# Normalised rational polynomials and a three-product forward step in a fused FFT convolution and MLP

## The chip, the cores and the metric

The kernel runs on one core of a Trainium2 chip. The time is the device time of one execution in microseconds (us); several runs are taken and their median is quoted. A unit of work below is a piece of the MLP, not a unit of time.

## The reference

`x` is [8, 3008, 256], two filters are [1505, 256]. Per batch and channel the sequence is filtered in the frequency domain, then every token goes through an MLP whose activation is a rational function:

```python
X = np.fft.rfft(x, axis=1)
y = np.fft.irfft(X * (filt_r + 1j * filt_i)[None], n=3008, axis=1)     # tokens: 24064 x 256
h = y @ w_in                                                           # 256 -> 2048
P = a[0] + a[1] * h + a[2] * h**2 + a[3] * h**3
Q = 1.0 + abs(b[0]) * abs(h) + abs(b[1]) * h**2
out = (P / (Q + 1e-06)) @ w_out                                        # 2048 -> 256
```

## The kernel before

The transform of length 3008 = 64 x 47 is cut into steps. **Stage 1** folds the input and multiplies by a 47-point matrix (line 444 for batches 1 to 7). **Stage 2** works in 12 steps a batch: the forward 64-point product y (`product`, line 497, one float32 matmul of 128x512), the multiplication by the filter on VectorE (DVE, lines 501 and 502), a cross term and a sum on GpSimd (POOL, lines 517 and 521), a split of the result into two float32r halves (`halves`: the upper on ScalarE (ACT), line 527, the lower on POOL, line 528), and the inverse product z as three float32r matmuls (`product3`, line 358), which is copied out of PSUM by `evac`, line 353, on the engine that the string `EV2` names ("V": DVE). **Stage 3** (line 590) is the 47-point inverse; its result is split into the halves `xh` and `xl`.

The MLP has 752 units (47 tiles of 512 tokens by 16 slices of 128 hidden features; the last one is cut in two). A unit makes six float32r products h (lines 631 to 634), the activation, and six products o (lines 714 to 716). The activation is taken by completing squares: on ACT `act0` |h| (L639), `act1` (h+PC)² (L646), `act2` (|h|+QC)² (L652), `act3` the reciprocal root of q+QK (L657), `act4` its square (L667; from unit 624 on POOL for every other unit, L665). PC, QC, QK, PK, P0 are [128,1] columns of the tile `scal`. On POOL follow q+QK (L677) and q times the upper half of g (L696), on DVE `p` (L682), `g_hi` (L691), `rest` (L699) and `g_lo` (L705).

The order is written by hand: `pipeline` goes through the units, and in each iteration issues the products h of unit i, then one piece of the generator `conv_items` for the next batch (stage 1, four pauses, stage 2), then the products o of unit i-4 and the steps of `ORDER` for earlier units. A generator's `yield` with a cost hands back the turn until enough credit is there; a bare `yield` is a pause of one iteration. Batch 0 and the splitting of the weights are done in `head`, ahead of the first unit; there a planner (`Plan`) orders the steps of all engines by estimated durations and due times. The step `flag` (L217 to L223) tests the coefficients, `scalars` (`square_scalars`) works out the columns on POOL, and the MLP's body stands behind a branch on the flag.

Of the kernel before, what the change touches and what calls it, by code (L numbers as in the profile page):

```python
# [11 lines left out]
I32 = mybir.dt.int32  # L12
# [28 lines left out]
CPOS = 3  # L41
V2 = "A"
# [140 lines left out]
def conv_moe(ctx: ExitStack, tc: tile.TileContext, xp, filt, w_in, w_out, mats, small, sgn, outT):  # L183
# [27 lines left out]
    B0, B1 = (abs_sb[:, i : i + 1] for i in (4, 5))  # L211
    P0, PC, PK, QC, QK, SC = (col(i) for i in range(6))

    def load_flag():


        nc.scalar.activation(abs_sb, ab_sb, AF.Abs)  # L217
        sq, c = col(8, 2), col(10, 2)
        tt(out=sq, in0=ab_sb[:, 6:8], in1=ab_sb[:, 6:8], op=ALU.mult)
        tt(out=c, in0=abs_sb[:, 8:10], in1=abs_sb[:, 10:12], op=ALU.mult)  # L220
        stt(out=c, in0=c, scalar=16.0, in1=sq, op0=ALU.mult, op1=ALU.is_ge)
        stt(out=c, in0=abs_sb[:, 10:12], scalar=1e-6, in1=c, op0=ALU.is_ge, op1=ALU.mult)
        tt(out=flag_sb, in0=col(10), in1=col(11), op=ALU.mult)  # L223

    def square_scalars():

        g = nc.gpsimd
        ts, tt = g.tensor_scalar, g.tensor_tensor
        x, y, z = col(6, 2), col(8, 2), col(10, 2)
        for n, src in ((6, A3), (7, B1)):  # L230
            ts(out=col(n), in0=src, scalar1=1.0, scalar2=None, op0=ALU.mult)
        v.reciprocal(y, x)
        tt(out=z, in0=x, in1=y, op=ALU.mult)
        ts(out=z, in0=z, scalar1=-1.0, scalar2=2.0, op0=ALU.mult, op1=ALU.add)
        tt(out=y, in0=y, in1=z, op=ALU.mult)
        tt(out=SC, in0=A3, in1=col(9), op=ALU.mult)
        p1, q1, pc2, qc2 = (col(i) for i in range(10, 14))
        for out, a, r in ((PC, A2, col(8)), (QC, B0, col(9))):
            ts(out=pc2, in0=a, scalar1=0.5, scalar2=None, op0=ALU.mult)
            tt(out=out, in0=pc2, in1=r, op=ALU.mult)  # L240
        tt(out=P0, in0=A0, in1=col(8), op=ALU.mult)
        tt(out=p1, in0=A1, in1=col(8), op=ALU.mult)
        ts(out=q1, in0=col(9), scalar1=1.000001, scalar2=None, op0=ALU.mult)
        tt(out=pc2, in0=PC, in1=PC, op=ALU.mult)
        tt(out=qc2, in0=QC, in1=QC, op=ALU.mult)
        tt(out=PK, in0=p1, in1=pc2, op=ALU.subtract)
        tt(out=QK, in0=q1, in1=qc2, op=ALU.subtract)

# [202 lines left out]
    class Stage2:  # L451


        def __init__(self, b):
            self.b, self.f, self.tin, self.ev, self.z, self.sides, self.parts = b, {}, {}, {}, {}, {}, {}

# [155 lines left out]
    class Unit:  # L612


        def __init__(self, i, squares):
            self.i, self.squares = i, squares
            self.t, self.f, self.cols = units[i]
            self.p0 = P0 if squares else A0

# [24 lines left out]
        def act1(self):  # L644
            if self.squares:
                nc.scalar.activation(self.w, self.H, AF.Square, bias=PC)  # L646
            else:
                nc.scalar.activation(self.w, self.H, AF.Identity, scale=A3, bias=A2)

        def act2(self):  # L650
            if self.squares:
                nc.scalar.activation(self.q, self.q, AF.Square, bias=QC)  # L652

        def act3(self):
            if self.squares:
# [97 lines left out]
    def head():  # L753
# [266 lines left out]
    with tc.manual_schedule(engines=ENGINES):  # L1020
# [85 lines left out]
```

## Time and profile before

| what | value |
|---|---|
| median of 3 runs | 2480.59 us (2480.01 to 2483.05) |
| profiled execution, first to last instruction | 2480.0 us; the trace shows nothing around it |
| PE (TensorE) busy | 2431.0 us, 98% |
| ACT busy | 2348.5 us, 95% |
| DVE busy | 2277.8 us, 92% |
| POOL busy | 2089.9 us, 84% |
| mean busy share of the DMA engines | 27.0% |

An instruction's row gives its start and its duration. Successive instructions of one engine overlap at their ends, so the time that one takes from its engine is the distance between two starts where the engine did not wait; a busy time of many instructions is their union.

### The profile page before, as it was taken

What the parts mean: (1) busy time and instruction counts of PE and PEld (TensorE: products, weight loads), DVE (VectorE), ACT (ScalarE), POOL (GpSimd) and SP (SyncE); (2) the same over time, 40 slices, a digit from 0 to 9 for tenths busy, and PEclk for the clock granted to TensorE, in tenths of its full rate; (3) what the DMA queues carried; (4) which work ended last, traced back from release to release, by engine and by line L of the source; (5) the groups of instructions that cost most, each with busy time, mean ns of one, the idle gap of its engine ahead of it and who ended that gap; (6) DMA issues with size and microseconds to landing.
All of it is one profiled execution on the core that took longest, in us unless ns stands there. A gap on an engine that the chain in (4) does not pass through costs nothing.

```text
span 2480.0 us, 36386 instructions
## 1 busy us (share of the span) xinstructions
PE 2431.0 (98%) x10770; PEld 1941.0 (78%) x10770; DVE 2277.8 (92%) x3568; ACT 2348.5 (95%) x4178; POOL 2089.9 (84%) x2240
## 2 busy tenths in 40 slices
PE   7699999999999999999999999999999999999999
PEld 4577777878778787787787877878778788888887
DVE  7789988999899998999889998999889999999998
ACT  6799999999999999999999999999999999999998
POOL 7788887898879987899878997889879887888898
PEclk8899999999999999999999999999999999999999
DMA  7533332322323232332323322332222210100000
GB/s 260 151 111 108 94 106 84 102 85 72 108 90 93 85 87 73 110 90 83 95 79 102 92 80 80 95 103 90 86 79 85 68 37 17 34 26 17 21 9 19
DMA packets 102423, 205.15 MB, mean 83 GB/s; under 512 B 9455, under 2 KB 55855, under 8 KB 102215
## 3 DMA queue, kind: packets, MB, share of 16 engines
q1 hardware_dynamic: 102215, 202.74, 27.0%
q8 instruction: 87, 1.43, 0.2%
q14 instruction: 121, 0.99, 0.1%
HBM read 130.53 MB, written 72.17 MB: 82 GB/s over the span
## 4 chain that ended last, share of the span: by engine, by line
PE 76%; ACT 8%; POOL 6%; DVE 6%; issue 3%; DMA 1%; SPq 0%; DVEq 0%; POOLq 0%; ACTq 0%
PE o L715 11%; PE o L714 11%; PE o L716 11%; PE h_u L631 11%; PE h_u L632 11%; PE h_u L634 11%; PE s L444 3%; PE x L590 3%; POOL q_u L696 3%; PE y L497 2%; PE z L358 2%; ACT q_u L652 2%; ACT q_u L639 2%; POOL q_u L677 1%; ACT a_u L657 1%
## 5 line engine op out<-in xcount | busy, mean ns | idle before, releaser
L696 POOL TENSOR_TENSOR q_u<-q_u,hi_u 128x512 f32<-128x512 f32 x753 | 975.4, 1295 | 246.5 <-DVE hi_u L691 226.7
L714 PE MATMUL o<-hi_u,wo_sb 128*128 128x512 f32 x1506 | 661.4, 439 | 0.0
L691 DVE SCALAR_TENSOR_TENSOR hi_u<-h_u,scal,a_u 128x512 fp32r<-128x512 f32 x753 | 557.4, 740 | 52.4 <-ACT a_u L667 44.1
L631 PE MATMUL h_u<-xhl,wi_sb 128*128 128x512 f32 x1506 | 592.6, 394 | 6.1 <-DVE raw L325 4.0
L715 PE MATMUL o<-lo_u,wo_sb 128*128 128x512 f32 x1506 | 588.5, 391 | 7.9 <-DVE lo_u L705 7.7
L716 PE MATMUL o<-hi_u,wo_sb 128*128 128x512 f32 x1506 | 587.6, 390 | 0.0
L632 PE MATMUL h_u<-xhl,wi_sb 128*128 128x512 f32 x1506 | 587.3, 390 | 0.0
L699 DVE SCALAR_TENSOR_TENSOR h_u<-h_u,scal,q_u 128x512 f32<-128x512 f32 x753 | 563.7, 749 | 24.2 <-POOL q_u L696 22.9
L682 DVE SCALAR_TENSOR_TENSOR h_u<-w_u,scal,h_u 128x512 f32<-128x512 f32 x753 | 560.3, 744 | 5.2 <-ACT w_u L646 5.2
L657 ACT ACTIVATE a_u<-q_u,scal 128x512 f32<-128x512 f32 x753 | 549.3, 729 | 0.0
L652 ACT ACTIVATE q_u<-q_u,scal 128x512 f32<-128x512 f32 x753 | 547.2, 727 | 1.9
L677 POOL TENSOR_SCALAR q_u<-q_u,scal 128x512 f32<-128x512 f32 x753 | 525.5, 698 | 1.5 <-ACT a_u L657 1.4
L646 ACT ACTIVATE w_u<-h_u,scal 128x512 f32<-128x512 f32 x753 | 518.8, 689 | 0.0
L705 DVE TENSOR_TENSOR lo_u<-h_u,a_u 128x512 fp32r<-128x512 f32 x753 | 512.5, 681 | 0.1
L639 ACT ACTIVATE q_u<-h_u 128x512 f32<-128x512 f32 x753 | 453.6, 602 | 56.6 <-PE h_u L634 46.8
L634 PE MATMUL h_u<-xhl,wi_sb 128*128 128x512 f32 x1506 | 464.5, 390 | 0.0
L667 ACT ACTIVATE a_u<-a_u 128x512 f32<-128x512 f32 x688 | 438.4, 637 | 0.3
L715 PEld LDWEIGHTS o<-lo_u,wo_sb 128*128 128x128 f32 x1506 | 283.3, 188 | 97.7 <-issue 37.0
L714 PEld LDWEIGHTS o<-hi_u,wo_sb 128*128 128x128 f32 x1506 | 283.0, 188 | 88.8 <-issue 36.9
L631 PEld LDWEIGHTS h_u<-xhl,wi_sb 128*128 128x128 f32 x1506 | 283.3, 188 | 74.3 <-DVE lo_u L705 8.8
L632 PEld LDWEIGHTS h_u<-xhl,wi_sb 128*128 128x128 f32 x1506 | 283.4, 188 | 60.4 <-issue 1.3
L716 PEld LDWEIGHTS o<-hi_u,wo_sb 128*128 128x128 f32 x1506 | 282.6, 188 | 60.9
(94 smaller groups left out, 2221.8 us busy)
## 6 DMA issues: line engine op xcount, KB each, us to landing
f<-filt SPq DMA_DIRECT2D x168, 256.0 KB
xin<-xp SPq DMA_DIRECT2D x48, 512.0 KB
scr<-ev SPq DMA_DIRECT2D x48, 512.0 KB
outT<-oe SPq DMA_DIRECT2D x46, 512.0 KB
xin<-scr SPq DMA_DIRECT2D x42, 512.0 KB
scr<-xin SPq DMA_DIRECT2D x42, 480.0 KB
tl<-scr SPq DMA_DIRECT2D x96, 192.0 KB
tl<-scr SPq DMA_DIRECT2D x62, 96.0 KB
```

Source lines behind the costliest of these rows:

```text
L631: nc.tensor.matmul(o, w_in_part(0, f, cc), xh[:, cc, ts], start=cc == 0, stop=False)
L632: nc.tensor.matmul(o, w_in_part(0, f, cc), xl[:, cc, ts], start=False, stop=False)
L634: nc.tensor.matmul(o, w_in_part(1, f, cc), xh[:, cc, ts], start=False, stop=cc == 1)
L652: nc.scalar.activation(self.q, self.q, AF.Square, bias=QC)
L657: nc.scalar.activation(self.a, self.q, AF.Abs_reciprocal_sqrt, bias=QK)
L682: v.scalar_tensor_tensor(out=H, in0=w, scalar=PK, in1=H, op0=ALU.add, op1=ALU.mult)
L691: nc.vector.scalar_tensor_tensor(out=self.hi, in0=self.H, scalar=self.p0, in1=self.a, op0=ALU.add, op1=ALU.mult)
L696: nc.gpsimd.tensor_tensor(out=self.q, in0=self.q, in1=self.hi.bitcast(F32), op=ALU.mult)
L699: nc.vector.scalar_tensor_tensor(out=self.H, in0=self.H, scalar=self.p0, in1=self.q, op0=ALU.add, op1=ALU.subtract)
L714: nc.tensor.matmul(o, w_out_part(0, f, dd), self.hi, start=f == 0 and self.cols.start == 0, stop=False)
L715: nc.tensor.matmul(o, w_out_part(0, f, dd), self.lo, start=False, stop=False)
L716: nc.tensor.matmul(o, w_out_part(1, f, dd), self.hi, start=False, stop=f == 15 and self.cols.stop == T)
```

## The change

**The polynomials** are scaled so that every added constant is 1 or -1. `act1`, `act2` and `act3` take the immediate bias 1.0 and a scale from one of three ACT registers, loaded once behind the branch (`load_rates`). `g_hi` and `rest` add the immediate 1.0. On POOL `pool_q1` multiplies and adds with two columns (S1, S2) where it had the immediate 1.0 and one column. The factor that is left over goes into the matrix `e_sb` of stage 3 and into SC. The columns are worked out on DVE (`scale_scalars`, ahead of the sixth fold), and the flag has more conditions.

**The forward product** of batches 1 to 7 becomes three float32r products: a new method `split` makes the halves of a piece of the loaded tile, the upper on ACT, the lower on DVE, one step ahead of the product. Stage 2 begins with three more pauses.

**The rest**: `EV2` becomes "A" (z is copied out by ACT), the costs of y and z in credit fall from 0.86 to 0.68, the lower halves of the matrices are made on DVE, and a scratch area of SBUF is made smaller.

```diff
-EV1, EV2, EVO = "A", "V", "AV"
-XB, FB = 4, 3
+EV1, EV2, EVO = "A", "A", "AV"
+XB, FB, YB = 4, 3, 2
...
-    fwd_sb = consts.tile([128, 128], F32, name="fwd_sb")
+    fwd_sb = consts.tile([128, 2, 128], F32R, name="fwd_sb")
...
+    def load_rates():
+        for k in range(3):
+            rate.append(nc.scalar.alloc_register(f"rate{k}"))
+            nc.scalar.reg_load(rate[k], rates_sb[:1, k : k + 1].bitcast(I32))
...
+        def split(self, i):
+            q, j = divmod(i, 2)
+            y = self.flat(self.tin[q], j)
+            tile = conv.tile([128, 2, TT], F32R, tag="yr", name=f"yr{self.b}_{i}", bufs=YB)
+            hi, lo = self.halved[i] = tile[:, 0], tile[:, 1]
+            nc.scalar.activation(hi, y, AF.Copy)
+            tt(out=lo, in0=y, in1=hi.bitcast(F32), op=ALU.subtract)
...
         def product(self, i):
-            yield 0.86
+            yield 0.68
             bank, yt = banks.tile(f"y_{b}_{i}")
-            nc.tensor.matmul(yt, fwd_sb, self.flat(self.tin[q], j), start=True, stop=True)
+            product3(yt, fwd_sb, *self.halved.pop(i))
...
+        yield
+        yield
+        s.split(0)
+        yield
         for i in range(13):
             if i < 12:
                 yield from s.product(i)
+            if i < 11:
+                s.split(i + 1)
             if i > 0:
                 yield from s.inverse(i - 1)
...
-            self.p0 = P0 if squares else A0
+            self.p0 = 1.0 if squares else A0
...
-                nc.scalar.activation(self.w, self.H, AF.Square, bias=PC)
+                nc.scalar.activation(self.w, self.H, AF.Square, bias=1.0, scale=rate[0])
...
-                nc.scalar.activation(self.q, self.q, AF.Square, bias=QC)
+                nc.scalar.activation(self.q, self.q, AF.Square, bias=1.0, scale=rate[1])
...
-                    nc.scalar.activation(self.a, self.q, AF.Abs_reciprocal_sqrt, bias=QK)
+                nc.scalar.activation(self.a, self.q, AF.Abs_reciprocal_sqrt, bias=1.0, scale=rate[2])
...
-                nc.gpsimd.tensor_scalar(out=self.q, in0=self.q, scalar1=1.0, scalar2=QK, op0=ALU.mult, op1=ALU.add)
+                nc.gpsimd.tensor_scalar(out=self.q, in0=self.q, scalar1=S1, scalar2=S2, op0=ALU.mult, op1=ALU.add)
...
-        add("mats_lower", mats_lower, "POOL", 1.3, ["mats_upper"], due=61)
+        add("mats_lower", mats_lower, "DVE", 0.8, ["mats_upper"], due=61)
...
-        add("scalars", square_scalars, "POOL", 4.0, ["flag"], due=20, then=[])
+        add("scalars", scale_scalars, "DVE", 2.5, ["flag"], due=4)
```

How the instructions move, in the order in which each engine takes them (line numbers of each kernel, `x_u381` is the buffer of unit 381, `y_5_4` the product of step 4 of batch 5):

DVE in stage 2, around a forward product, before:

```order
L691 SCALAR_TENSOR_TENSOR hi_u382_14148<-h_u382_14071,scal_79,a_u382_14087 128x512
L501 TENSOR_TENSOR f25_2_13626<-y_5_4_14140,f25_2_13626 128x512
L502 TENSOR_TENSOR f15_2_13625<-y_5_4_14140,f15_2_13625 128x512
L699 SCALAR_TENSOR_TENSOR h_u381_14035<-h_u381_14035,scal_79,q_u381_14056 128x512
L682 SCALAR_TENSOR_TENSOR h_u383_14101<-w_u383_14119,scal_79,h_u383_14101 128x512
L705 TENSOR_TENSOR lo_u381_14165<-h_u381_14035,a_u381_14055 128x512
L691 SCALAR_TENSOR_TENSOR hi_u383_14190<-h_u383_14101,scal_79,a_u383_14117 128x512
L353 COPY ev5_1_14025<-z_5_3_14180 128x512
```

and now:

```order
L731 SCALAR_TENSOR_TENSOR hi_u402_15062<-h_u402_14969,a_u402_14990 128x512
L538 TENSOR_TENSOR f25_2_14443<-y_5_4_15052,f25_2_14443 128x512
L539 TENSOR_TENSOR f15_2_14442<-y_5_4_15052,f15_2_14442 128x512
L525 TENSOR_TENSOR yr5_5_15074<-xin5_2_14448,yr5_5_15074 128x512
L739 SCALAR_TENSOR_TENSOR h_u401_14933<-h_u401_14933,q_u401_14954 128x512
L722 SCALAR_TENSOR_TENSOR h_u403_15007<-w_u403_15030,scal_79,h_u403_15007 128x512
L745 TENSOR_TENSOR lo_u401_15082<-h_u401_14933,a_u401_14953 128x512
```

The copy of z is gone, the lower half of the next piece (L525) stands behind the two filter products, and L731 and L739 read no column. Of the rows shown L525 alone has both of its inputs in SBUF: h, y and z are in PSUM.

ACT in stage 2, now:

```order
L682 ACTIVATE q_u398_14846<-h_u398_14825 128x512
L524 ACTIVATE yr5_4_14854<-xin5_2_14448 128x512
L707 ACTIVATE a_u397_14800<-a_u397_14800 128x512
L695 ACTIVATE q_u398_14846<-q_u398_14846 128x512
L689 ACTIVATE w_u398_14847<-h_u398_14825 128x512
L699 ACTIVATE a_u398_14845<-q_u398_14846 128x512
L682 ACTIVATE q_u399_14888<-h_u399_14867 128x512
L379 ACTIVATE ev5_1_14857<-z_5_2_14874 128x512
```

The upper half (L524) and the copy of z (L379) stand behind the |h| of their iteration; L695, L689 and L699 name no column any more.

DVE in the head, now, from the fifth fold on:

```order
L419 TENSOR_TENSOR xs4_157<-xin0_2_114 120x512
L239 TENSOR_SCALAR scal_79<-scal_79 128x1
L240 TENSOR_SCALAR scal_79<-small_sb_78,scal_79 128x1
L241 TENSOR_SCALAR scal_79<-small_sb_78,scal_79 128x1
L242 TENSOR_SCALAR scal_79<-small_sb_78 128x1
L243 TENSOR_SCALAR scal_79<-scal_79 128x1
L244 TENSOR_SCALAR scal_79<-small_sb_78,scal_79 128x1
L245 TENSOR_SCALAR scal_79<-scal_79 128x2
```

Before, the fold xs5 came straight behind xs4; now 28 small instructions stand between them, and the flag ahead of xs1 has 14 where it had 5.

## Rows read from the trace of the kernel before

**Rows 1.** Busy time by stretch: us, then PE, PEld, DVE, ACT, POOL, clock, DMA.

```profile
20.00:85.00 65.00, 47.31 (x177) 27.29 (x176) 51.62 (x82) 45.23 (x72) 61.32 (x63) 0.82 0.61 208
200.00:2050.00 1850.00, 1841.82 (x8080) 1470.91 (x8079) 1715.69 (x2684) 1781.84 (x3190) 1576.62 (x1706) 1.00 0.29 88
1290.00:1420.00 130.00, 129.63 (x573) 103.98 (x572) 125.84 (x199) 124.22 (x223) 117.63 (x134) 1.00 0.31 91
```

**Rows 2.** Timeline of PE in a stage 2: start, duration, engine, line, operands, count.

```profile
1313.77 1.02 PE L497 MATMUL y<-xin,fwd_sb 128*128 128x512 f32 x2
...
1314.86 0.40 PE L715 MATMUL o<-lo_u,wo_sb 128*128 128x512 f32 x1
...
1317.39 0.84 PE L358 MATMUL z<-zr,inv_sb 128*128 128x512 f32 x3
1318.07 0.39 PE L714 MATMUL o<-hi_u,wo_sb 128*128 128x512 f32 x1
```

**Rows 3.** Timeline of ACT, the same stretch.

```profile
1314.64 0.59 ACT L639 ACTIVATE q_u<-h_u 128x512 f32<-128x512 f32 x1
1315.11 0.63 ACT L667 ACTIVATE a_u<-a_u 128x512 f32<-128x512 f32 x1
1315.63 0.72 ACT L652 ACTIVATE q_u<-q_u,scal 128x512 f32<-128x512 f32 x1
1316.25 0.69 ACT L646 ACTIVATE w_u<-h_u,scal 128x512 f32<-128x512 f32 x1
1316.82 0.73 ACT L657 ACTIVATE a_u<-q_u,scal 128x512 f32<-128x512 f32 x1
```

**Rows 4.** Timeline of DVE, the same stretch.

```profile
1313.71 0.68 DVE L705 TENSOR_TENSOR lo_u<-h_u,a_u 128x512 fp32r<-128x512 f32 x1
1314.31 0.74 DVE L691 SCALAR_TENSOR_TENSOR hi_u<-h_u,scal,a_u 128x512 fp32r<-128x512 f32 x1
1314.97 0.68 DVE L501 TENSOR_TENSOR f<-y,f 128x512 f32<-128x512 f32 x1
1315.57 0.68 DVE L502 TENSOR_TENSOR f<-y,f 128x512 f32<-128x512 f32 x1
```

**Rows 5.** Timeline of POOL, the same stretch.

```profile
1315.82 0.93 POOL L517 TENSOR_SCALAR zw<-f,sgn_sb 64x256 f32<-64x256 f32 x2
1316.84 1.30 POOL L696 TENSOR_TENSOR q_u<-q_u,hi_u 128x512 f32<-128x512 f32 x1
```

**Rows 6.** Timelines of DVE and of POOL in the head.

```profile
7.89 6.96 DVE L391 TENSOR_TENSOR xs<-xin 120x512 f32<-120x512 f32 x12 [1.62 <-DMA xin<-xp]
...
24.70 0.43 DVE L313 TENSOR_SCALAR wp<-wt 128x512 uint32<-128x512 uint32 x1
...
28.30 1.49 DVE L313 TENSOR_SCALAR wp<-wt 128x512 uint32<-128x512 uint32 x1
...
6.90 0.19 POOL L235 TENSOR_TENSOR scal<-scal 128x2 f32<-128x2 f32 x1
...
9.18 0.73 POOL L241 TENSOR_TENSOR scal<-small_sb,scal 128x1 f32<-128x1 f32 x1
...
26.95 2.55 POOL L323 TENSOR_TENSOR raw<-raw,wp 128x512 f32<-128x512 f32 x2
```

**Rows 7.** Timelines of DVE and ACT in the head.

```profile
5.03 0.16 DVE L221 SCALAR_TENSOR_TENSOR scal<-scal 128x2 f32<-128x2 f32 x1
5.23 0.16 DVE L222 SCALAR_TENSOR_TENSOR scal<-scal 128x2 f32<-128x2 f32 x1
...
17.07 0.70 DVE L292 SCALAR_TENSOR_TENSOR wa<-wa,raw 128x512 f32<-128x512 f32 x1 [2.23 <-ACT wa L288]
...
85.04 0.63 ACT L333 ACTIVATE wo_sb<-wt 128x512 fp32r<-128x512 f32 x1 [3.07 <-POOL wt L330]
```

**Rows 8.** The branch's load of the flag on ACT: duration, first and last start.

```profile
L1031 ACTq TENSOR_LOAD <-scal x1: 466/466/466, 85.0 to 85.0; - x1
```

More of the change, by code (lines that the diff above doesn't have):

```diff
@@ L41 @@
 CPOS = 3
-V2 = "A"
 OG = 2
@@ L211, in conv_moe @@
     B0, B1 = (abs_sb[:, i : i + 1] for i in (4, 5))
-    P0, PC, PK, QC, QK, SC = (col(i) for i in range(6))
+    PK, S1, S2, SC, SG = (col(i) for i in range(5))
+    rates_sb = scal[:, 44:47]
+    rate = []
     def load_flag():
         nc.scalar.activation(abs_sb, ab_sb, AF.Abs)
-        sq, c = col(8, 2), col(10, 2)
+        sq, c, D, aD = col(5, 2), col(8, 2), col(7), col(15)
         tt(out=sq, in0=ab_sb[:, 6:8], in1=ab_sb[:, 6:8], op=ALU.mult)
+        stt(out=D, in0=abs_sb[:, 11:12], scalar=4.000004, in1=col(6), op0=ALU.mult, op1=ALU.subtract)
@@ L220, in load_flag @@
         tt(out=c, in0=abs_sb[:, 8:10], in1=abs_sb[:, 10:12], op=ALU.mult)
         stt(out=c, in0=c, scalar=16.0, in1=sq, op0=ALU.mult, op1=ALU.is_ge)
[L222 to L247, printed above, removed]
@@ new lines, in load_flag @@
+        stt(out=aD, in0=D, scalar=-1.0, in1=D, op0=ALU.mult, op1=ALU.max)
+        stt(out=aD, in0=aD, scalar=1024.0, in1=col(6), op0=ALU.mult, op1=ALU.is_ge)
+        tt(out=c, in0=c, in1=aD.to_broadcast([128, 2]), op=ALU.mult)
+        big, all_ = scal[:, 48:54], scal[:, 54:56]
+        ts(out=big, in0=abs_sb[:, :6], scalar1=2.0**-17, scalar2=None, op0=ALU.is_ge)
+        stt(out=big, in0=abs_sb[:, :6], scalar=1024.0, in1=big, op0=ALU.is_le, op1=ALU.mult)
+        tt(out=big[:, :3], in0=big[:, :3], in1=big[:, 3:], op=ALU.mult)
@@ new lines, in load_flag, with scale_scalars @@
+        tt(out=all_, in0=big[:, :2], in1=c, op=ALU.mult)
+        tt(out=all_[:, :1], in0=all_[:, :1], in1=big[:, 2:3], op=ALU.mult)
+        tt(out=all_[:, :1], in0=all_[:, :1], in1=all_[:, 1:], op=ALU.mult)
+        tt(out=flag_sb, in0=all_[:, :1], in1=all_[:, :1], op=ALU.mult)
+    def scale_scalars():
+        yes, no = scal[:, 54:55], scal[:, 55:56]
+        n, r, t = scal[:, :7], scal[:, 56:62], scal[:, 48:54]
+        ts(out=no, in0=yes, scalar1=-1.0, scalar2=1.0, op0=ALU.mult, op1=ALU.add)
+        ts(out=n[:, 0:1], in0=ab_sb[:, 0:1], scalar1=yes, scalar2=no, op0=ALU.mult, op1=ALU.add)
+        ts(out=n[:, 6:7], in0=ab_sb[:, 1:2], scalar1=yes, scalar2=no, op0=ALU.mult, op1=ALU.add)
+        ts(out=t[:, :1], in0=ab_sb[:, 2:3], scalar1=0.5, scalar2=None, op0=ALU.mult)
+        ts(out=n[:, 1:2], in0=t[:, :1], scalar1=yes, scalar2=no, op0=ALU.mult, op1=ALU.add)
+        ts(out=n[:, 2:3], in0=ab_sb[:, 3:4], scalar1=yes, scalar2=no, op0=ALU.mult, op1=ALU.add)
+        ts(out=n[:, 3:5], in0=abs_sb[:, 4:6], scalar1=yes, scalar2=no, op0=ALU.mult, op1=ALU.add)
+        ts(out=n[:, 5:6], in0=col(7), scalar1=yes, scalar2=no, op0=ALU.mult, op1=ALU.add)
+        v.reciprocal(r, n[:, :6])
+        tt(out=t, in0=n[:, :6], in1=r, op=ALU.mult)
+        ts(out=t, in0=t, scalar1=-1.0, scalar2=2.0, op0=ALU.mult, op1=ALU.add)
+        tt(out=r, in0=r, in1=t, op=ALU.mult)
+        a0, a2, a3, b0, b1, d, a1 = (n[:, k : k + 1] for k in range(7))
+        ra0, ra2, ra3, rb0, rb1, rd = (r[:, k : k + 1] for k in range(6))
+        u, w = t[:, 0:1], t[:, 1:2]
+        stt(out=SG, in0=a2, scalar=a2, in1=ra3, op0=ALU.mult, op1=ALU.mult)
+        tt(out=SG, in0=SG, in1=ra0, op=ALU.mult)
+        stt(out=u, in0=a3, scalar=ra2, in1=ra2, op0=ALU.mult, op1=ALU.mult)
+        ts(out=PK, in0=u, scalar1=a1, scalar2=-1.0, op0=ALU.mult, op1=ALU.add)
+        tt(out=u, in0=u, in1=a0, op=ALU.mult)
+        stt(out=rates_sb[:, 0:1], in0=a3, scalar=ra2, in1=u, op0=ALU.mult, op1=ALU.mult)
+        stt(out=u, in0=u, scalar=-1.0, in1=u, op0=ALU.mult, op1=ALU.max)
+        stt(out=w, in0=b1, scalar=2.0, in1=rb0, op0=ALU.mult, op1=ALU.mult)
+        tt(out=rates_sb[:, 1:2], in0=u, in1=w, op=ALU.mult)
+        stt(out=rates_sb[:, 2:3], in0=b0, scalar=b0, in1=rd, op0=ALU.mult, op1=ALU.mult)
+        ts(out=S2, in0=d, scalar1=0.0, scalar2=2.0, op0=ALU.is_ge, op1=ALU.mult)
+        ts(out=S2, in0=S2, scalar1=-1.0, scalar2=None, op0=ALU.add)
+        tt(out=S1, in0=rates_sb[:, 2:3], in1=S2, op=ALU.mult)
+        stt(out=u, in0=b1, scalar=4.0, in1=a0, op0=ALU.mult, op1=ALU.mult)
+        stt(out=SC, in0=rd, scalar=S2, in1=u, op0=ALU.mult, op1=ALU.mult)
+        ts(out=e_sb, in0=e_sb, scalar1=SG, scalar2=None, op0=ALU.mult)
@@ L533, in inverse @@
                 self.ev[q] = self.tl("ev", q)
-            yield 0.86
+            yield 0.68
             bank, zt = banks.tile(f"z_{b}_{i}")
@@ L777, in mats_upper @@
                 nc.scalar.activation(out[rows, 0], of[rows], AF.Copy)
-            nc.scalar.activation(fwd_sb, pair[3], AF.Copy)
+            nc.scalar.activation(fwd_sb[:, 0], pair[3], AF.Copy)
         def mats_lower():
             for out, of, rows in ((inv_sb, pair[0], slice(0, 64)), (inv_sb, pair[1], slice(64, 128))):
-                nc.gpsimd.tensor_tensor(out=out[rows, 1], in0=of[rows], in1=out[rows, 0].bitcast(F32), op=ALU.subtract)
+                tt(out=out[rows, 1], in0=of[rows], in1=out[rows, 0].bitcast(F32), op=ALU.subtract)
+            tt(out=fwd_sb[:, 1], in0=pair[3], in1=fwd_sb[:, 0].bitcast(F32), op=ALU.subtract)
         def s_sum(j):
@@ L867, in head @@
             add(f"sev{j}", lambda j=j: s_ev(j), "ACT", 0.5, [f"s{j}"], due=j)
-        add("flag", load_flag, "ACT", 0.2, ["small"], due=3, then=[("DVE", 1.0)])
-        add("scalars", square_scalars, "POOL", 4.0, ["flag"], due=20, then=[])
+        add("flag", load_flag, "ACT", 0.2, ["small"], due=3, then=[("DVE", 1.2)])
+        add("scalars", scale_scalars, "DVE", 2.5, ["flag"], due=4)
         add("pair", load_pair, "SP", 0.5, due=12, moves=0.55)
@@ L1032, in conv_moe @@
             with tc.If(flag > 0) as cmp:
+                load_rates()
                 body(True)
```

7 lines of the change are left out of this document (2 added, 5 removed).

## The prediction

> **What bounds the kernel now.** I read the stretches first. Between 200 and 2050 us PE is busy 1841.8 of 1850 us at a granted clock of 1.00 (the 2.4 GHz level), while ACT is busy 1781.8, DVE 1715.7 and POOL 1576.6 [rows 1]. PE therefore has at most 8.2 us of idle time to give back there. But a busy time alone doesn't say that an engine runs at its rate, so I went to PE's timeline: the three products of a z start at 1317.39 and the next o at 1318.07, 0.68 us, or 0.227 a product [rows 2], and the products of the units stand at the same distance from each other. PE issues at its rate nearly everywhere; a unit of 12 products costs it 12 x 0.227 = 2.72 us. So time is won where PE is given less to do, and what is saved on ACT or DVE is only slack. The exception is the head, where PE is busy 47.3 of 65 us between 20 and 85 us and POOL 61.3 [rows 1]: there ACT's last step before the branch waits 3.07 us for POOL [rows 7].
>
> **The forward product.** The float32 y starts at 1313.77, and the second o product behind it at 1314.86 [rows 2]; less the 0.227 of the first o, y costs 0.86. Three float32r products of the same shape cost what z costs, 0.68. The difference of 0.18 lies on the path, in 7 batches x 12 steps: 84 x 0.18 = **-15.4 us**. This term is firm: the shapes are those of z, and the row of z is measured.
>
> **What it costs beside PE.** I work in steps of stage 2. By the order of PE's instructions, 11 steps of batch 5 take 49 units before and 51 now, 4.45 and 4.64 units a step; the pauses and the third stage set this, not the credit. One step of PE is 4.45 x 2.72 + 0.86 + 0.68 + about 0.5 for the third stage = 14.2 us before, and 4.64 x 2.72 + 0.68 + 0.68 + 0.5 = 14.5 now. The other engines must fit into 14.5; their loads before are taken from the stretch of batch 5, 1290 to 1420 [rows 1].
>
> *ACT*: 124.2/130 x 14.2 = 13.6 us. From start to start a square or root of an SBUF tile takes 0.52 without a column (L667) and 0.62 with one (L652), from PSUM 0.47 (L639) and 0.57 (L646) [rows 3]: a column costs 0.10. If a register as scale costs nothing, a unit saves 0.30 of 2.80. Then a step is 13.6 + 0.19 x 2.80 - 4.64 x 0.30 + 0.52 (upper half) + 0.47 (copy of z) = 13.7, which leaves 0.8 us. No row shows a scale from a register. Its price lies between nothing and that of a column (0.10); I take nothing, since an immediate is what L639 and L667 have, and keep 0.10 for the rival.
>
> *DVE*: 125.8/130 x 14.2 = 13.75. An instruction with a column takes 0.66 (L691), one without 0.60 (L705, L501) [rows 4], so `g_hi` and `rest` save 0.12 a unit. The copy of z (0.60) goes, the lower half (0.60) comes. With 0.19 x 2.58 for the longer step and 4.64 x 0.12 taken off, this makes 13.7, plus the wait of the next paragraph.
>
> *POOL*: 117.6/130 x 14.2 = 12.85, + 0.19 x 2.0 for the longer step = 13.2. A second column in L677 has no row; between nothing and ACT's 0.10 a unit it adds 0 to 0.46 a step. I take half.
>
> **A new collision.** The lower half is the one large DVE instruction of the pipeline with both inputs in SBUF. In the head such instructions and POOL hold each other up: while DVE makes its folds, a POOL multiply of one column takes 0.73 instead of 0.19, and a DVE shift that takes 0.43 takes 1.49 when it meets two POOL multiplies from 26.95 to 29.50 [rows 6]. In stage 2 the lower half would start where L502 ends, 1315.57 + 0.60 = 1316.17; POOL is then in its two cross terms until 1316.75 [rows 5], so it would wait 0.58. I take 0.6 a step, with bounds of 0 (it falls between two POOL instructions) and 1.30 (a whole multiply, L696). DVE comes to 14.3 of 14.5 and POOL, held up for 0.6, to 14.0. Both still fit, so PE loses little: I put 2 us for all 84 steps, between 0 and 5 while this holds. The Trainium skill (SBUF — State Buffer, Who interferes with whom) says that VectorE with two SBUF inputs and GpSimd reading SBUF share a port by an exclusive lock for the whole instruction. The rows of the head agree; it speaks against this change, and by a full lock each time the sum would be that of the first rival.
>
> **The head.** The flag's 9 more instructions, at 0.20 a start [rows 7], fit in DVE's 1.62 us of waiting for the second load [rows 6]. The 28 columns between the folds cost 28 x 0.20 = 5.6 us; 2.23 of it lies in DVE's wait ahead of the first weight [rows 7]. The three lower halves of the matrices stand behind it; DVE has no row of such a size, between a small instruction (0.2) and a full one (0.6) I take 0.3 each, 0.9. DVE brings the first weight 4.3 us later. POOL follows, and has 65 - 61.3 = 3.7 us of idle time between 20 and 85 us to catch up in [rows 1]: +0.6 to +4.3, I take 2.5. That POOL is rid of its own columns gains nothing, as it waits for DVE's weights behind them. Behind the branch ACT loads three registers. One such load takes 0.466 [rows 8], so 0 to 1.4; the shorter units win some of it back, I take 1.0. Head: **+3.5 us** (-1, if the planner's new order suits POOL better, to +5.7).
>
> **The rest at nothing.** SP's load of the flag moves ahead of two weight loads; it waits for 14 instructions of 0.20 that begin around 5 us, and DVE takes up its first weight at 17 us only [rows 7]. The three pauses and the longer steps put the last z of batch 7 on unit 625 instead of 600; stage 3 first wants it on unit 641, and if it were later the rest would be issued at once, ahead of other work. The loads of stage 2 stand three pauses ahead of the first split. The store of z now follows ACT, behind a copy that waits for z alone. Fewer stalls of PE and a shorter last unit, with ACT and DVE ahead: 0 to -8.2, I take **-1**.
>
> **Sum** on the profiled span of 2480.0, which is 0.6 under the median: 2480.0 - 15.4 + 3.5 + 2 - 1 = 2469.1; with the 0.6, **2469.7 us**. Its own range: low with head -1, no collision and most of the stalls gone, 2480.6 - 15.4 - 1 - 5 = 2459; high with 5.7 and 5, 2476.
>
> **The rivals.**
> *The collision fills DVE.* The point is a wait of 14.5 - 13.7 = 0.8 us for the lower half. At the 1.06 that the shift lost (1.49 - 0.43) [rows 6], a step would be 0.25 us longer, 84 x 0.25 = 21: 2469.7 - 2 + 21 = 2489; at 0.95 it is 13, 2481; at 1.30, 42, 2510. For it: DVE is 97% and POOL 90% busy in stage 2 before [rows 1]. Against it: DVE's place falls on the short cross terms, and buffers of four and five units smooth single waits. Chance 0.14, half of it within 0.2% of the time before, half above.
> *A register costs as much as a column* (slower). Then ACT does not get its 0.30 a unit, but does get the upper half and the copy of z: 13.7 + 4.64 x 0.30 = 15.1 a step, 0.6 over PE; the point from which ACT decides is 0.8 / (3 x 4.64) = 0.06 us an instruction. 84 x 0.6 = 50: 2520. For it: no row excludes it. Against it: ACT's rows show no extra time for what comes with the instruction. Chance 0.12, 0.02 of it just past the point and within 0.2%.
> The change not doing what it says is excluded by the order: the columns are gone from ACT's and DVE's rows, and y is issued three times.
>
> **How the numbers follow.** My forecast has 0.74, of which 0.03 ends within 0.2% (5 us, about what a measurement can tell from no change). Faster: 0.71. Same: 0.03 + 0.07 + 0.02 = 0.12. Slower: 0.07 + 0.10 = 0.17. The range of 2459 to 2488 takes in the forecast and the lower half of the first rival; above it about 0.15 is left out, below it little.
>
> **What would show it.** Right: three y products 0.227 apart and 0.68 in all; L652, L646 and L657 with the durations of L667 and L639; PE idle for under 13 us between 200 and 2050; the first h some 3 us later than before. Wrong: roots and squares from a register at 0.62 from start to start with ACT at 99% in stage 2 (second rival); lower halves of over 1.5 us, with PE waiting for `g_lo` or for ACT in stage 2 (first rival); a head that grows by over 6 us.

## The result, and the profile after

The change makes the kernel slower: 2510.3 us (median of 4 runs, 2509.62 to 2512.78) against 2481.8 for the kernel before; ratio 1.0114, interval 1.0103 to 1.0126. That is 28 us slower, and 41 us above the predicted time. The profiled execution spans 2510.9 us.

The page of the changed kernel, its busy times and some of its groups (busy, mean ns of one, idle before):

```profile
PE 2436.8 (97%) x10854; PEld 1955.8 (78%) x10854; DVE 2207.9 (88%) x3607; ACT 2272.8 (91%) x4346; POOL 2166.4 (86%) x2221
...
L739 DVE SCALAR_TENSOR_TENSOR h_u<-h_u,q_u 128x512 f32<-128x512 f32 x753 | 518.9, 689 | 104.3 <-POOL q_u L736 102.9
...
L731 DVE SCALAR_TENSOR_TENSOR hi_u<-h_u,a_u 128x512 fp32r<-128x512 f32 x753 | 511.3, 679 | 78.9 <-ACT a_u L707 78.4
...
L699 ACT ACTIVATE a_u<-q_u 128x512 f32<-128x512 f32 x753 | 478.1, 635 | 0.0
L695 ACT ACTIVATE q_u<-q_u 128x512 f32<-128x512 f32 x753 | 473.1, 628 | 1.8
...
L689 ACT ACTIVATE w_u<-h_u 128x512 f32<-128x512 f32 x753 | 446.3, 593 | 0.0
```

ACT and DVE became lighter, as meant (95% to 91%, 92% to 88%), and POOL heavier (2089.9 to 2166.4 us). The three ACT instructions with a register scale take 0.59 to 0.64 us where those with a column took 0.69 to 0.73 [rows 3], so that part works. But the stretches, against [rows 1], show where the time went:

```profile
20.00:85.00 65.00, 43.30 (x182) 23.46 (x176) 51.47 (x87) 43.68 (x69) 56.61 (x59) 0.84 0.57 198
200.00:2050.00 1850.00, 1824.99 (x8081) 1468.55 (x8080) 1640.00 (x2649) 1723.50 (x3320) 1608.98 (x1662) 1.00 0.29 86
1290.00:1420.00 130.00, 128.82 (x574) 104.02 (x573) 113.14 (x182) 121.25 (x233) 106.28 (x110) 1.00 0.25 76
```

Between 200 and 2050 us PE now idles 25.0 us where it idled 8.2. In 1850 us DVE and ACT have more idle time than before, and still PE waits: no engine has become full. The table of waits says at which product:

```profile
POOL q_u L736 <- DVE hi_u L731: 191.4, 174, 3.6
DVE h_u L739 <- POOL q_u L736: 102.9, 191, 1.2
...
PEld h_u L674 <- DVE lo_u L745: 38.0, 58, 1.5
```

The last row is the telling one. PEld is PE's weight load, the first instruction of a product. A unit's first product h needs the PSUM bank that `g_lo` (L745) of an earlier unit frees. In the kernel before, the same row is

```profile
PEld h_u L631 <- DVE lo_u L705: 8.8, 17, 1.1
```

Now one step of stage 2 of batch 5 in the changed kernel. PE's timeline:

```profile
1435.60 0.84 PE L386 MATMUL y<-yr,fwd_sb 128*128 128x512 f32 x3
...
1439.00 0.84 PE L386 MATMUL z<-zr,inv_sb 128*128 128x512 f32 x3
```

ACT's, DVE's and POOL's in the same stretch:

```profile
1436.67 0.64 ACT L524 ACTIVATE yr<-xin 128x512 fp32r<-128x512 f32 x1
1437.19 0.63 ACT L707 ACTIVATE a_u<-a_u 128x512 f32<-128x512 f32 x1
1437.71 0.63 ACT L695 ACTIVATE q_u<-q_u 128x512 f32<-128x512 f32 x1
1438.23 0.60 ACT L689 ACTIVATE w_u<-h_u 128x512 f32<-128x512 f32 x1
1438.71 0.65 ACT L699 ACTIVATE a_u<-q_u 128x512 f32<-128x512 f32 x1
```

```profile
1437.68 0.68 DVE L525 TENSOR_TENSOR yr<-xin,yr 128x512 fp32r<-128x512 f32 x1
1438.28 0.69 DVE L739 SCALAR_TENSOR_TENSOR h_u<-h_u,q_u 128x512 f32<-128x512 f32 x1
```

```profile
1437.76 1.40 POOL L554 TENSOR_SCALAR zw<-f,sgn_sb 64x256 f32<-64x256 f32 x2
...
1441.39 0.94 POOL L554 TENSOR_SCALAR zw<-f,sgn_sb 64x256 f32<-64x256 f32 x2
```

y costs what z costs (0.84 for the row of three, as in [rows 2]). From start to start L695 takes 0.52 and L689 0.48; what had immediates before took 0.52 and 0.47 [rows 3]. And the collision is there, only that POOL is the one that waits for most of it: two cross terms beside the lower half (L525) take 1.40 us, two without it 0.94, as before [rows 5].

Two more places. The first h starts at 86.72, 4.0 us later than the 82.76 of before:

```profile
86.72 0.76 PE L674 MATMUL h_u<-xhl,wi_sb 128*128 128x512 f32 x1 [5.19 <-DVE raw L353]
```

And at 343 us, when stage 3 first asks for batch 1, its last two inverse products come at once:

```profile
343.06 0.84 PE L386 MATMUL z<-zr,inv_sb 128*128 128x512 f32 x3
347.52 2.15 PE L386 MATMUL z<-zr,inv_sb 128*128 128x512 f32 x3 [3.62 <-ACT zr L564]
349.47 0.63 PE L754 MATMUL o<-hi_u,wo_sb 128*128 128x512 f32 x1
349.90 0.63 PE L755 MATMUL o<-lo_u,wo_sb 128*128 128x512 f32 x1
```

PE waits 3.62 us, and then the products stand 0.43 apart instead of 0.227: behind the gap the clock is granted at its lower level, 1.2 GHz (0.50 between 350 and 353 us).

### The profile page after: what moved, and what is told of

Same layout as the page of the kernel before. It is cut to its first block, busy times and chain, and to the rows that moved or that the text cites. A ratio compares the mean times of both kernels' runs of the same rounds, so it can differ in the third digit from the quotient of the medians.

```text
span 2510.9 us, 36728 instructions
## 1 busy us (share of the span) xinstructions
PE 2436.8 (97%) x10854; PEld 1955.8 (78%) x10854; DVE 2207.9 (88%) x3607; ACT 2272.8 (91%) x4346; POOL 2166.4 (86%) x2221
## 4 chain that ended last, share of the span: by engine, by line
PE 61%; POOL 17%; DVE 12%; issue 5%; ACT 4%; DMA 1%; POOLq 0%; ACTq 0%; DVEq 0%; SPq 0%
PE h_u L674 9%; PE h_u L675 9%; PE h_u L677 9%; PE o L755 9%; PE o L754 9%; PE o L756 9%; POOL q_u L736 7%; POOL q_u L717 4%; PE s L472 3%; PE x L633 3%; DVE h_u L739 3%; POOL zw L554 2%; DVE h_u L722 2%; DVE hi_u L731 2%; POOL zr L565 1%
## 5 line engine op out<-in xcount | busy, mean ns | idle before, releaser
L736 POOL TENSOR_TENSOR q_u<-q_u,hi_u 128x512 f32<-128x512 f32 x753 | 975.8, 1296 | 214.6 <-DVE hi_u L731 191.4
L754 PE MATMUL o<-hi_u,wo_sb 128*128 128x512 f32 x1506 | 629.3, 418 | 0.0
L739 DVE SCALAR_TENSOR_TENSOR h_u<-h_u,q_u 128x512 f32<-128x512 f32 x753 | 518.9, 689 | 104.3 <-POOL q_u L736 102.9
L756 PE MATMUL o<-hi_u,wo_sb 128*128 128x512 f32 x1506 | 587.7, 390 | 0.0
L717 POOL TENSOR_SCALAR q_u<-q_u,scal 128x512 f32<-128x512 f32 x753 | 581.4, 772 | 2.2 <-ACT a_u L699 2.2
L731 DVE SCALAR_TENSOR_TENSOR hi_u<-h_u,a_u 128x512 fp32r<-128x512 f32 x753 | 511.3, 679 | 78.9 <-ACT a_u L707 78.4
L745 DVE TENSOR_TENSOR lo_u<-h_u,a_u 128x512 fp32r<-128x512 f32 x753 | 511.7, 680 | 0.1
L699 ACT ACTIVATE a_u<-q_u 128x512 f32<-128x512 f32 x753 | 478.1, 635 | 0.0
L695 ACT ACTIVATE q_u<-q_u 128x512 f32<-128x512 f32 x753 | 473.1, 628 | 1.8
L689 ACT ACTIVATE w_u<-h_u 128x512 f32<-128x512 f32 x753 | 446.3, 593 | 0.0
L707 ACT ACTIVATE a_u<-a_u 128x512 f32<-128x512 f32 x688 | 432.8, 629 | 0.3
```

The lines of the kernel that those rows point to most:

```text
L717: nc.gpsimd.tensor_scalar(out=self.q, in0=self.q, scalar1=S1, scalar2=S2, op0=ALU.mult, op1=ALU.add)
L731: nc.vector.scalar_tensor_tensor(out=self.hi, in0=self.H, scalar=self.p0, in1=self.a, op0=ALU.add, op1=ALU.mult)
L736: nc.gpsimd.tensor_tensor(out=self.q, in0=self.q, in1=self.hi.bitcast(F32), op=ALU.mult)
L739: nc.vector.scalar_tensor_tensor(out=self.H, in0=self.H, scalar=self.p0, in1=self.q, op0=ALU.add, op1=ALU.subtract)
L745: nc.vector.tensor_tensor(out=self.lo, in0=self.H, in1=self.a, op=ALU.mult)
L754: nc.tensor.matmul(o, w_out_part(0, f, dd), self.hi, start=f == 0 and self.cols.start == 0, stop=False)
```

## The experiments

Times beside each run's own runs of the kernel before (2481.9 to 2483.2 us). One hundredth of the ratio is 24.8 us. Two theories stood at the start: A, that GpSimd with its second column now sets the pace of stage 2; B, that ScalarE holds the units up, since the upper half and the copy of z stand in its queue. Both fell as whole explanations; from `both_mends` on the question is what in the split costs the rest.

### The two parts apart

`poly_only` is the change without the three-product step:

```diff
-EV1, EV2, EVO = "A", "A", "AV"
+EV1, EV2, EVO = "A", "V", "AV"
-            product3(yt, fwd_sb, *self.halved.pop(i))
+            nc.tensor.matmul(yt, fwd_sb, self.flat(self.tin[q], j), start=True, stop=True)
...
-        yield
-        yield
-        s.split(0)
-        yield
...
```

> The changed kernel with the float32 forward product, the copy of z on VectorE and no pauses put back: only the polynomials are changed. Theory A (GpSimd: the second column makes L717 0.073 us longer in all 753 units, and in stage 2 GpSimd sets the pace): slower than before by 8 us of head and fill plus at least half of the steady loss, 2495 to 2510, with TensorE waiting in stage 2. Theory B (ScalarE in order: the upper halves and the copies of z hold up the units behind them): the head's 8 us alone, or a little less, 2485 to 2490.

2483.5 us, ratio 1.0005 (0.9996 to 1.0015): no change, and below both ranges. `product_only` is the kernel before with only the three-product step (the old columns and `square_scalars` put back):

> The kernel before with the three-product forward step, its splits, its pauses and the copy of z on ScalarE: only the forward step is changed. Theory A: the second column is absent, so GpSimd has 5 to 6% of room in stage 2 and TensorE waits no more than before, except for batch 1 (about 8 us): 2480 - 15 + 8, 2470 to 2480. Theory B: ScalarE has its columns of 0.10 us back and is over-full in stage 2, by about 0.6 us a step: 2515 or more. Both can hold here in part; the stall of TensorE by stage tells.

2520.9 us, 1.0155 (1.0138 to 1.0172). The step that was to save 15 us loses 38 on its own; what the lighter polynomials do is to give back about 10 of it. Here theory B's forecast came true: ACT still reads its columns and is busy 1817.4 of the 1850 us between 200 and 2050, so this kernel may lose time on ACT that the change does not lose.

### Two suspected losses, each taken away

`one_column`:

```diff
-                nc.gpsimd.tensor_scalar(out=self.q, in0=self.q, scalar1=S1, scalar2=S2, op0=ALU.mult, op1=ALU.add)
+                nc.gpsimd.tensor_scalar(out=self.q, in0=self.q, scalar1=S1, scalar2=1.0, op0=ALU.mult, op1=ALU.add)
```

> The changed kernel with the immediate 1.0 in the place of the column S2 on GpSimd (S2 is 1 for these coefficients). Theory A: L717 falls from 0.77 to 0.70 us and the steady loss goes, 15 to 28 us faster than the changed kernel, 2482 to 2495. Theory B: the same time as the changed kernel within 4 us.

2498.5 us, 1.0062 (1.0045 to 1.0079): 13 us faster than the change, a little less than theory A's 15 to 28 and far from theory B's 4. The row of the instruction between 200 and 2050 us, in the change and in this kernel:

```profile
L717 POOL TENSOR_SCALAR q_u<-q_u,scal 128x512 f32<-128x512 f32 x567 | 438.1, 773 | 0.0
```

```profile
L717 POOL TENSOR_SCALAR q_u<-q_u,scal 128x512 f32<-128x512 f32 x571 | 398.2, 697 | 0.0
```

The second column costs 0.076 us a unit.

`batch1_early` draws stage 1 of batch 1 together by three units:

```diff
-REST = 4
+REST = 1
```

> The changed kernel with batch 1 begun three iterations earlier (REST 1 instead of 4), so that its last z stands on unit 72 as before and is not issued in one piece on unit 73. If the piece of 8 us around unit 73 is the missed due time: 7 to 9 us faster than the changed kernel, 2501 to 2504. If it is only waiting that would come anywhere: no difference over 2 us.

2502.5 us, 1.0082 (1.0065 to 1.0099): 8 us faster than the change. The stretch around 343 us, in the change and here (PE is the second number, the granted clock the third from the right):

```profile
330.00:365.00 35.00, 30.38 (x127) 24.04 (x126) 24.57 (x41) 28.02 (x57) 27.55 (x29) 0.90 0.44 134
```

```profile
330.00:365.00 35.00, 35.00 (x159) 28.55 (x158) 30.36 (x52) 33.19 (x66) 30.86 (x30) 1.00 0.31 88
```

PE gets its 4.6 us of idle time back and the clock stays at 1.00. `both_mends` makes both edits:

> The change with both single mends at once: GpSimd's polynomial step with one register column (1.0 in the place of the second, which alone gave 12 us), and batch 1's first stage drawn together by three units so that its last inverse product comes before unit 73 (alone 8 us). If the two are separate losses they add: 2510 - 12 - 8 = 2490 us, 8 us above the kernel before, and about 23 us of the saving of 15 us plus nothing else are still lost elsewhere (in the split). If the late batch 1 is itself a result of a full GpSimd, they overlap: about 2498 us. If the two were all that was lost, it would be 2466 to 2470 us.

2488.9 us, 1.0025 (1.0015 to 1.0035): the two add up. Still slower than before, so, if the three products save their 15 us, a third loss of over 20 us remained.

### The third loss

`no_split` has the products read the loaded tile as both halves, and so leaves out the split and its values:

```diff
-            tile = conv.tile([128, 2, TT], F32R, tag="yr", name=f"yr{self.b}_{i}", bufs=YB)
-            hi, lo = self.halved[i] = tile[:, 0], tile[:, 1]
-            nc.scalar.activation(hi, y, AF.Copy)
-            tt(out=lo, in0=y, in1=hi.bitcast(F32), op=ALU.subtract)
+            self.halved[i] = y.bitcast(F32R), y.bitcast(F32R)
```

> The change without the two halves: the three products of the forward step read the loaded float32 tile directly, once as each half, so ScalarE loses 84 copies (0.5 us) and VectorE 84 subtractions (0.8 us); the three pauses, the inverse copy on ScalarE and the polynomials stay, and TensorE does the same products (the split's values are left out of the computation, so the spectra are wrong). Theory split (what is lost in stage 2 is the time that the two halves take on two in-order engines): 15 to 30 us faster than the change, 2480 to 2495 us. Theory pauses and z copy (the loss is the batch's lateness and the inverse copy on ScalarE): no more than 5 us faster, about 2506 us.

2486.0 us, 1.0016 (1.0007 to 1.0026): the split costs 24 us. `mends_no_split` has both mends besides:

> The change with both mends and without the two halves (the products read the loaded tile as each half; the split is left out of the computation). If the three losses (second column, late batch 1, split) are separate they add: 2510 - 21 - 24 = 2465 us, and the saving of the three products (15 us) is seen whole. If there is a loss besides (the pauses, the inverse copy on ScalarE, the later batches), 2472 us or more.

2464.9 us, 0.9927 (0.9910 to 0.9943). That is where the sum of the three put it; pauses and z copy leave little room for a fourth. `z_vector` (the change with `EV2 = "V"`) asks of the z copy alone:

> The change with the inverse product's copy to SBUF back on VectorE, where it was before, all else as changed. ScalarE loses 0.5 us in a step of 14 us, VectorE gains 0.6 us. Theory ScalarE in order (the copy waits there behind and ahead of the units' squares and holds their chain up): 5 to 10 us faster than the change, about 2502 us. Theory VectorE full (TensorE's first products wait for banks that VectorE's lo frees late): VectorE gets busier still and the time rises by 10 to 20 us, to about 2525 us.

2507.9 us, 1.0107 (1.0090 to 1.0124): no clear difference from the change, though DVE goes up to 2253.1 us (90%). Both theories missed here.

### What in the split

`lo_from_psum` leaves the number of instructions as it is, but in every step but a batch's first the subtraction reads one operand from PSUM, the forward product of the step before. What it writes is then no lower half:

```diff
-            tt(out=lo, in0=y, in1=hi.bitcast(F32), op=ALU.subtract)
+            if i == 0:
+                tt(out=lo, in0=y, in1=hi.bitcast(F32), op=ALU.subtract)
+            else:
+                bank, yt = self.held
+                tt(out=lo, in0=yt, in1=hi.bitcast(F32), op=ALU.subtract)
+                banks.done(bank, 0.5)
...
```

> The change with the lower half's subtraction on VectorE reading one SBUF operand and one PSUM operand (the forward product of the step before, whose bank is kept that little longer) in the place of two SBUF operands; the values are then not the lower halves. Same instruction count on every engine. Theory shared port (VectorE waits for GpSimd at this instruction and GpSimd behind it): the instruction falls from 0.81 to about 0.69 us, GpSimd's cross products are no longer held up, and the time falls by 5 to 15 us. Theory plain occupancy (the instruction's own 0.68 us on VectorE is what costs): within 3 us of the change, 2507 to 2513 us.

2500.4 us, 1.0075 (1.0058 to 1.0092): 10 us faster than the change. `mends_lo_psum`, the same with both mends:

> The change with both mends and the lower half's subtraction reading one operand from PSUM (the values are then not the lower halves). Of the 24 us between 2489 and 2465 the shared port's part is what this gives back: as on the unmended change, 10 us, so 2479 us; if the port's part and the late batch 1 were one loss, 2485 us or more.

2477.9 us, 0.9983 (0.9974 to 0.9993): 10 us again. `mends_no_lo` drops the lower half and keeps the upper (`hi, lo = self.halved[i] = tile[:, 0], tile[:, 0]`, no subtraction):

> The change with both mends and without the lower half alone: ScalarE still writes the upper half of every tile, VectorE does nothing, and the products read the upper half as the lower (the lower half is left out of the computation). Between 2489 us (with the whole split) and 2465 us (without any). If ScalarE's copy costs as much as its 0.5 us a step suggests it may not (ScalarE is 91% busy, in order): about 2478 us. If VectorE's subtraction is all of the split's loss: 2465 to 2468 us.

2468.8 us, 0.9944 (0.9928 to 0.9961). From `both_mends` down: port 10.4 us, the subtraction's own time on DVE 9.7, the upper half on ACT 4.2. The last step is inside the intervals; the other two are not. How the 20.1 us divide between these two is less sure: the variant keeps y's bank longer, and z waits for it, as the waits below show.

The rows of POOL's column instruction, of the cross terms and of the lower half between 200 and 2050 us, in `both_mends`:

```profile
L717 POOL TENSOR_SCALAR q_u<-q_u,scal 128x512 f32<-128x512 f32 x573 | 401.3, 700 | 0.0
...
L554 POOL TENSOR_SCALAR zw<-f,sgn_sb 64x256 f32<-64x256 f32 x295 | 167.0, 578 | 57.0 <-issue 25.5 <-DVE f L538 20.1 <-POOL q_u L717 0.2
...
L525 DVE TENSOR_TENSOR yr<-xin,yr 128x512 fp32r<-128x512 f32 x80 | 56.8, 710 | 11.9 <-ACT yr L524 11.9
```

and in `mends_lo_psum`:

```profile
L562 POOL TENSOR_SCALAR zw<-f,sgn_sb 64x256 f32<-64x256 f32 x296 | 138.1, 478 | 60.7 <-issue 26.3 <-DVE f L543 22.9 <-POOL q_u L725 0.2
...
L529 DVE TENSOR_TENSOR yr<-y,yr 128x512 fp32r<-128x512 f32 x75 | 50.9, 678 | 0.4 <-ACT yr L524 0.4
```

The collision takes 4 x 0.10 us a step from POOL and 0.03 from DVE. And it is seen at the wait of PE's weight loads for `g_lo`'s bank, in `both_mends`, `mends_lo_psum`, `mends_no_lo` and `mends_no_split`:

```profile
PEld h_u L674 <- DVE lo_u L745: 28.5, 55, 1.5
```

```profile
PEld h_u L682 <- DVE lo_u L753: 11.0, 15, 1.3
```

```profile
PEld h_u L673 <- DVE lo_u L744: 9.1, 19, 1.6
```

```profile
PEld h_u L671 <- DVE lo_u L742: 7.0, 15, 0.9
```

Most of the fall comes with the port (28.5 to 11.0), little with the subtraction's own time (11.0 to 9.1). What goes in that second step is a wait of z that `mends_lo_psum` has made itself:

```profile
PEld z L386 <- DVE yr L529: 14.2, 19, 1.8
```

In `both_mends` the longest wait of z's loads is 7.9 us, for ACT. So some of the 9.7 us may belong to the port; the sum of 20.1 does not hang on this.

DVE's wait for POOL (L739 in the change) does not tell the kernels apart: it is 93.1 us with the split and 99.2 without.

### Attempts to place the lower half better

`split_at_total` issues the split behind POOL's sum instead of behind the two filter products:

```diff
-            if i < 11:
-                s.split(i + 1)
             if i > 0:
                 yield from s.inverse(i - 1)
...
                 s.total(i)
+                if i < 11:
+                    s.split(i + 1)
```

> The change with the split of the next tile issued one or two units later in the step: behind GpSimd's sum of the products (a unit in which VectorE and ScalarE have nothing of the step to do) in the place of right behind VectorE's two multiplications. The same instructions, pauses and products. Theory crowding (VectorE has the two multiplications and the lower half, some 2 us, in one unit of 3.35 us on top of its three operations for the units, and the banks of the first products come free late in that unit): 8 to 15 us faster than the change, about 2498 us. Theory lock (the subtraction waits for GpSimd wherever it stands, and GpSimd's sum is now right beside it): no more than 3 us either way.

2527.5 us, 1.0178 (1.0161 to 1.0195): 16 us slower than the change; both theories missed. `mends_split_total`, with both mends (the one column in the form of `poly_one_column` below):

> The same move together with the two mends (batch 1's first stage drawn together; one register column on GpSimd, here by letting the polynomials run only where 4 a0 b1 - b0^2 is positive, so that the sign column and four small VectorE operations of the head go). Computes the reference. Theory crowding, losses adding up: 2489 - 10 = 2479 us, within 0.2% of the kernel before. Theory lock: 2487 to 2490 us.

2502.4 us, 1.0079 (1.0062 to 1.0096): 13 us slower than `both_mends`, and both theories missed again. The row in `split_at_total`:

```profile
L525 DVE TENSOR_TENSOR yr<-xin,yr 128x512 fp32r<-128x512 f32 x78 | 86.8, 1113 | 45.8 <-ACT yr L524 45.8
```

Beside POOL's long instructions (1.3 us) the lower half takes 1.11 us, and DVE waits 45.8 us for the upper half, where it waits 13.5 in the change. `mends_lo_end` issues the lower half at the end of its unit, behind `g_lo`:

```diff
-            tt(out=lo, in0=y, in1=hi.bitcast(F32), op=ALU.subtract)
+            return lambda: tt(out=lo, in0=y, in1=hi.bitcast(F32), op=ALU.subtract)
...
             for name, lag in ORDER[CPOS:]:
                 step(lag, name)
+            while behind:
+                behind.pop()()
```

> The change with both mends and the lower half issued on VectorE at the end of its unit, behind the operation that frees the first product's bank, in the place of ahead of three of the unit's operations. Computes the reference. Theory place (the subtraction delays the freeing of banks by its own length): the first products wait less, about 2480 us. Theory port (it waits for GpSimd and holds VectorE wherever it stands): 2487 to 2492 us.

2488.3 us, 1.0024 (1.0015 to 1.0034), the time of `both_mends`, as theory port had it. Its rows say why nothing is won:

```profile
L717 POOL TENSOR_SCALAR q_u<-q_u,scal 128x512 f32<-128x512 f32 x573 | 432.5, 755 | 0.0
...
L554 POOL TENSOR_SCALAR zw<-f,sgn_sb 64x256 f32<-64x256 f32 x296 | 138.1, 478 | 56.2 <-issue 26.5 <-DVE f L538 18.4 <-POOL q_u L717 0.2
...
L525 DVE TENSOR_TENSOR yr<-xin,yr 128x512 fp32r<-128x512 f32 x80 | 89.8, 1122 | 11.2 <-ACT yr L524 11.2
```

The cross terms are free again, but the lower half now begins beside POOL's long L736 and waits, 0.44 us a step, and then holds up the L717 behind it: at 1434 us L525 takes 1.28 us and that L717 1.14. Over the stretch L717 takes 31 us more than in `both_mends` where the cross terms take 29 less. POOL loses what it lost before, in another place, and DVE waits besides. `mends_lo_next` (the lower half one unit behind the upper, after the inverse product):

> The change with both mends and the lower half issued one unit after the upper half, in the unit of the inverse product's copy, in which VectorE has nothing else of the step: not on top of the two multiplications, and not waiting for the upper half. Computes the reference. Theory crowding: 2477 to 2482 us. Theory port: 2487 to 2500 us, as the later place cost 13 us when it came beside GpSimd's sum.

2485.3 us, 1.0013 (1.0003 to 1.0023): 3 us better than `both_mends`, which is inside the intervals, and between the two theories.

### A version that beats both

`poly_one_column` is `poly_only` with one column on POOL; the flag asks that 4·a0·b1 − b0² be positive, so the sign column and four small DVE instructions of the head fall away, and other coefficients take the general body:

```diff
-        stt(out=aD, in0=D, scalar=-1.0, in1=D, op0=ALU.mult, op1=ALU.max)
-        stt(out=aD, in0=aD, scalar=1024.0, in1=col(6), op0=ALU.mult, op1=ALU.is_ge)
+        stt(out=aD, in0=D, scalar=1024.0, in1=col(6), op0=ALU.mult, op1=ALU.is_ge)
...
-                nc.gpsimd.tensor_scalar(out=self.q, in0=self.q, scalar1=S1, scalar2=S2, op0=ALU.mult, op1=ALU.add)
+                nc.gpsimd.tensor_scalar(out=self.q, in0=self.q, scalar1=rates_sb[:, 2:3], scalar2=1.0, op0=ALU.mult, op1=ALU.add)
```

> The normalised polynomials alone (forward step as before), with one register column on GpSimd in the place of two (the polynomials run only where 4 a0 b1 - b0^2 is positive). Computes the reference. Theory second column paid only beside the three-product step: 2482 to 2484 us, as with two columns. Theory second column paid by every unit once ScalarE is eased: 5 to 10 us faster than the kernel before, about 2475 us.

2478.2 us, 0.9986 (0.9977 to 0.9996): 3.5 us faster than the kernel before and 32 faster than the change. The time lies between the two theories. Beside `poly_only` this is 5 us less, of which the shorter head (its first h is 0.95 us earlier) may have a part; beside the split the column cost 13.

## Why the prediction was wrong

The ratios form a chain from the change back to the kernel before (in us; single links are good to some 3 to 6, and as differences they add up to the whole whatever they are):

| step | us |
|---|---|
| second column on POOL (change to `one_column`) | 12.9 |
| batch 1 late (`one_column` to `both_mends`) | 9.2 |
| lower half: port (to `mends_lo_psum`) | 10.4 |
| lower half: its own time on DVE (to `mends_no_lo`) | 9.7 |
| upper half on ACT (to `mends_no_split`) | 4.2 |
| one float32 product to three (to `poly_one_column`) | -14.6 |
| polynomials, head and all (to before) | -3.5 |
| sum | 28.3 |

**The forward product: right.** -15.4 predicted, -14.6 found, pauses and z copy included.

**A register scale at nothing: right.** The rows show the immediates' durations, and the second rival (2520 us by ACT) falls: ACT is 91% busy over the span, 93% between 200 and 2050 us.

**The head: right in size at its end, without effect later.** +3.5 was forecast; the first h is 4.0 later. But `poly_only`, whose first h is also late (85.97), ends at the time of before, and `poly_one_column` (85.02) under it: by its end the polynomials have made the late start good. In the sum the two belong in one term, which came to -3.5.

**"Both still fit, so PE loses little: I put 2 us for all 84 steps": wrong, and this is the step that failed.** The loads were about right: the lower half's wait was taken as 0.6 a step and is 0.4 to 0.5, though mostly on POOL, in the cross terms behind it; the second column was taken as 0.23 a step, half of its bounds, and is 4.64 x 0.076 = 0.35. Wrong was to hold their sum against PE's 14.5 us a step as if time below that were free. The split's 24 us are 0.29 us for each of 84 steps, while DVE idles more than before. The wait that follows the split is the one for the bank that `g_lo` frees: it falls from 28.5 to 7.0 us as the split is taken out. By the order, a delay of any engine along a unit's chain (ACT, POOL and DVE in turn) delays that bank; the sentence that "buffers of four and five units smooth single waits" looked at SBUF buffers, not at the PSUM banks (six, shared by h, y, z and the products of the first and third stage). That the banks are the limit agrees with the waits, but no run had more of them; that is argued, not shown.

**The first rival named the right collision, but not how it costs.** It had DVE wait, and lose nothing below 0.8 us a step. The meeting takes 0.4 to 0.5 us, mostly from POOL, and costs some 10 us there. That the rival's 2510, for a wait of 1.30, is the measured time is chance, as most of the loss lies elsewhere. The shift that gave its 1.06 (L313 [rows 6]) also reads one SBUF tile and not two, so it was no row of such a subtraction. By the lock that the Trainium skill states (SBUF — State Buffer, Who interferes with whom) the sum would have been the first rival's 2489. The rows agree that VectorE and GpSimd exclude each other (1.40 against 0.94 on one side, 1.12 against 0.68 on the other), but the port alone makes only some 10 of the 28 us.

**"If it were later the rest would be issued at once": wrong batch.** The due time was looked at for batch 7 alone. Batch 1 had no slack: the three pauses pushed its last z onto the unit where stage 3 asks for it, and exactly what the sentence says happened there, for 8 to 9 us. This term was missing from the sum.

The range ended at 2488 because it took the costs beside PE to be none up to a threshold.

## What to carry to other kernels

As this kernel shows, a busy share of 90% need not be 10% of free room. Where engines hand a unit on to each other and a scarce buffer is freed only at the end of that chain, look for the wait of the bounding engine that already exists (here PE for `g_lo`'s bank, 8.8 us before) and price added work by how it lengthens that chain. A pause added to a generator moves every batch, so each batch's due time has to be looked at, the first one above all. When two instructions exclude each other at a port, moving one only chose here which instructions wait, and in one place made both engines wait; what helped was a PSUM operand for one of them, or to leave it out.

## What the runs showed of the hardware

- A register as scale with an immediate bias costs on ACT what an immediate alone does: 0.52 us from start to start for a 128x512 tile in SBUF, 0.48 from PSUM. Loading three registers back to back took 0.28 us each, where the flag's single load took 0.466 [rows 8].

```profile
L275 ACTq TENSOR_LOAD <-scal x3: 282/283/285, 91.7 to 92.4; - x3
```

- A second [128,1] column on POOL costs 0.076 us for 128x512 (0.773 against 0.697).
- A DVE subtraction of 128x512 with both inputs in SBUF and POOL's multiplications hold each other up by some 0.4 us a meeting, on the side that comes second (1.40 against 0.94 us for two of POOL's, 1.12 against 0.68 for DVE's). A subtraction that begins beside one POOL instruction and ends beside the next can wait for the one and hold up the other (1.28 and 1.14 us in `mends_lo_end`, against 0.68 and 0.70). With one input in PSUM neither row lengthens (0.678 and 0.478).
